# Where the last slice of v, the bias split and batch 1's turns stand in a fused attention and mixer kernel

## The chip, the cores and the metric

One core of a Trainium2 chip runs the whole kernel. The metric is the time of one execution on the device in microseconds (us); three executions of the kernel before were timed, and one more was profiled.

## What is computed

Four batches of 576 tokens, 8 heads of 64: attention with a local mask (heads 0 to 3, the last 32 positions) and a strided mask (heads 4 to 7, every 32nd position), then a gated mixer, then a second mixer with sines and cosines. All in fp32 at the interface.

```python
scores = np.where(masks, scale * q @ k.T, -1e9)      # per head
x = softmax(scores) @ v                              # heads side by side: x is 576 x 512
h = np.maximum(x @ w_in, 0.0)
u, v = h[..., :512], h[..., 512:]
v_n = (v - mean(v)) / np.sqrt(var(v) + 1e-06)
v_s = einsum('ts,bsd->btd', w_spatial, v_n) + b_spatial[None, :, None]
x = (u * v_s) @ w_out
theta = x @ w_theta
y = einsum(w_tok_r, x * cos(theta)) + einsum(w_tok_i, x * sin(theta))
out = x + y + np.maximum((x + y) @ w_ch, 0.0)
```

## The kernel before

Numbers are split in two fp16 halves, high and low (`dst[0]`, `dst[1]`; `e` is the half), and each product is three matmuls, high by high, low by high and high by low (`PASS`). Weights arrive as raw 64-bit words and are converted in steps of two row blocks: a load, two casts on ACT, one operation on DVE, a cast to the high half on ACT and a subtraction for the low half on POOL or DVE (`from_f64`, `steps_w`, `part`).

Batch 0 opens alone with `attention0`: nine groups of score blocks pass through a pipeline of a few steps, `s`. A group is scored on PE (`gr_scores`), shifted on DVE (`gr_shift`: a maximum, TENSOR_REDUCE, and a subtraction, TENSOR_TENSOR), exponentiated on ACT (`gr_exp`), turned by PE transposes and copied by ACT (`gr_turn`, into `pT`), multiplied by v and divided (`gr_pv`), turned back and written to `xT` by ACT and DVE, high half and low half (`gr_out`, `gr_parts`). During this stage each engine takes its instructions in the order in which the code is written.

After it a scheduler sets the order on each engine from priorities, and the main products run in chunks. `main_v` makes v of x @ w_in: four blocks of 128 tokens in two pairs (`v0`, `v1`) and a tail of 64 tokens that PE makes as two halves (`v2`, `tail_mm`, `fold_tail`). `v_relu` evicts a pair or the tail on ACT and takes its statistics on DVE (BN_STATS); `norm` makes 1/sqrt(var) by twelve small DVE operations on the tile `rs` and scales; `norm_q` writes the halves of `vn`. `main_mid` makes four chunks of u (24 matmuls each), four of sp (the product with w_spatial: 24 matmuls and 4 with the tail rows and the bias), of x2 and of th; `main_end` makes y and c. PSUM gives the main chunks and the score tiles of batch 1 (`a`) one pool of three tiles (`pm`).

Batch 1's attention runs beside batch 0's main products. `attention1` is a generator: one step scores group s, sends it through maximum, subtraction and exponential, then turns group s-1 and divides group s. Whenever a main chunk yields, `others()` steps it if the count of main products so far (`now()`, in us of full-clock matmul time) has passed `ATT_AT[b]`, a start and a gap. So a step's instructions on PE (scores, turns, products with v) stand between two chunks, and the turn stands directly behind the scores, with no main products in between.

The last row of `wspt` holds the bias, split in two halves: `sp_tail` loads it behind the tail of w_spatial in `x2f`, and makes two ACT operations of one partition by 576 and one on DVE. `x2f` is afterwards the place of the second half of w_out.

Of the kernel before, what the change touches and what calls it, by code (L numbers as in the profile page):

```python
# [21 lines left out]
STRIDE = 32  # L22
# [12 lines left out]
LAG16 = 3  # L35
V_ORDER = (0, 1, 2)
E_WAY = 'aaaadaaadaa'
# [18 lines left out]
LEAD = 3.0  # L56
ATT_AT = (None, (2.7, 4.2), (86.0, 5.4), (174.5, 4.6))
PREP_AT = (112.0, 126.0, 131.0)
# [11 lines left out]
def kernel(  # L70
# [249 lines left out]
    def sp_tail():  # L320
        stg = pair(stage()[0].bitcast(F32), S)
        for j in range(2):
            nc.sync.dma_start(stg[j * TL:(j + 1) * TL, 0, :], w_spT[T0:S, :])
        nc.sync.dma_start(stg[TL:TL + 1, 1, :], b_sp)
        nc.sync.dma_start(stg[96:97, 1, :], b_sp)
        nc.scalar.activation(wspt[:, 0, :], stg[:, 0, :], AF.Copy, scale=SPS)
        nc.vector.scalar_tensor_tensor(wspt[0:TL, 1, :], stg[0:TL, 0, :], SPS, wspt[0:TL, 0, :],
                                       op0=ALU.mult, op1=ALU.subtract)
        nc.scalar.activation(wspt[TL:TL + 1, 1, :], stg[TL:TL + 1, 1, :], AF.Copy, scale=SPS)
        nc.scalar.activation(wspt[96:97, 1, :], stg[96:97, 1, :], AF.Copy, scale=SPS)  # L330
        nc.vector.scalar_tensor_tensor(wspt[96:97, 1, :], stg[96:97, 1, :], SPS, wspt[96:97, 1, :],
                                       op0=ALU.mult, op1=ALU.subtract)
# [296 lines left out]
    def gr_parts(b, local, blocks, xt, by=1):  # L629
# [3 lines left out]
        for i, (hp, blk) in enumerate(blocks):  # L633
            if runs and runs[-1][0] == hp and (local or blk < 10):
                runs[-1][3] += 1
            else:
                runs.append([hp, blk, i, 1])
        for hp, blk, i, n in runs:
            src = xt[:, QB * i:QB * (i + n)]
            if local:  # L640
                dst = [xh[:, e, hp, QB * blk:QB * (blk + n)] for e in range(2)]
# [11 lines left out]
    def attention0(aside):  # L653
# [12 lines left out]
        nc.scalar.activation(x2f[:, 0, 0:1], halfpi, AF.Exp)  # L666
        make_masks()
        load_qk(0, 0, q[0], k[0], 4 * QB, S)
        load_vl(0, 0, v[0])
# [8 lines left out]
        for s in range(NG + 3):  # L678
            mid, end = aside.get(s, ((), ()))
            if s < NG:  # L680
                if s % 4 == 3:
                    banks = pa("sc"), pa("av")
                else:
                    two = pm("at")
                    banks = two[:, 0, :], two[:, 1, :]
                t = s2("smx")
                sm, pT = t[:, 0, 0:384], t[:, 1, 0:512].rearrange("p (n k) -> p n k", n=4)
                st = att_p.tile([P, 2, 6], F32, tag="st", name="st", bufs=4)
                un[s] = banks, sm, pT, st
                gr_scores(s, q, k, banks[0])  # L690
                gr_shift(s, banks[0], sm, st)
# [125 lines left out]
    def attention1(b):  # L817
# [20 lines left out]
        for s in range(NQ + 2):  # L838
# [17 lines left out]
            if s in loads:  # L856
                f, hp = loads[s]
                f(hp)
            if 1 <= s < NQ:
                turn()  # L860
# [119 lines left out]
    def main_v(b):  # L980
# [43 lines left out]
        def v_mm(ps, i, c):  # L1024
            for n, (xe, we) in enumerate(PASS):
# [3 lines left out]
                    start=(c == 0 and n == 0), stop=(c == NC - 1 and n == 2)).ins.name))  # L1029

        if b == 0:
            ps = [pm("v0")]
# [13 lines left out]
            some(1, (2,))  # L1046
            yield
            for pr in range(2):
                some(pr, (3,))
                yield  # L1050
                v_relu(pr, ps[pr])
            norm((0, 1))
        for pr in V_ORDER if b else V_ORDER[2:]:
            ps = pm(f"v{pr}")
            if pr == 2:
                tail_mm(ps[:, 0, :], xh, win, slice(DM, 2 * DM))
                yield
            else:
                for t in range(2):
                    for c in range(NC):  # L1060
                        v_mm(ps[:, t, :], 2 * pr + t, c)
                    yield
            v_relu(pr, ps)
        norm((2,) if b == 0 else (0, 1, 2))

    def main_mid(b):
# [3 lines left out]
        def u_chunk(m):  # L1070
            ps = pm(f"u{m}")
            k = 0
            for c in range(NC):
                for we, xe in PASS:
                    mm2(ps, win[:, we, c, m * P:(m + 1) * P], xh[:, xe, c, :], k == 0, k == 3 * NC - 1)
                    k += 1
            u = s1(f"u{m}")
            ha.activation(fold(u), halves(ps), AF.Relu, scale=XS / (PS * SS))
            us[m] = u

        def sp_chunk(m):
# [3 lines left out]
            for c in range(NF):  # L1085
                for ve, we in PASS:
                    mm2(ps, vn[:, c, ve, d], wsp[:, we, c, :], k == 0, False)
                    k += 1
            mm2(ps, vn[:, 4, 0, d], wspt[:, 0, :], False, False)
            mm2(ps, k2[:, d], wspt[:, 1, :], False, True)  # L1090
# [4 lines left out]
        for f, m in ((u_chunk, 0), (u_chunk, 1), (u_chunk, 2), (sp_chunk, 0), (u_chunk, 3), (sp_chunk, 1),  # L1095
                     (sp_chunk, 2), (sp_chunk, 3)):
            f(m)
            yield
# [19 lines left out]
        for m in (2, 3):  # L1118
            ps = pm(f"x2{m}")
            x2_mm(m, ps, range(NC))  # L1120
            x2_evac(m, ps)
# [132 lines left out]
    att = {"b": 1, "n": 0}  # L1254

    def now():
        return clock[0] / 2400.0
# [9 lines left out]
    def others():  # L1267
        while conv and conv[0][0] <= now():
            conv.pop(0)[1]()
        while att["b"] < B and ATT_AT[att["b"]][0] + att["n"] * ATT_AT[att["b"]][1] <= now():  # L1270
            step()
# [18 lines left out]
    def go():  # L1290
# [11 lines left out]
        NG + 1: ((), (go, e2, a3, b3)),  # L1302
        NG + 2: ((), (go, c3, lambda: sp_part(0), e3, step, lambda: sp_part(2))),
    })
# [95 lines left out]
```

## Time and profile before

| | |
|---|---|
| time of three executions | 489.02, 491.31 and 491.95 us, median 491.31 |
| time of the profiled execution | 488.88 us |
| its span, first to last instruction | 487.0 us |
| PE busy | 467.9 us (96% of the span) |
| DVE, ACT, POOL busy | 300.2, 268.6, 72.4 us |
| granted TensorE clock, mean | 0.996 |

A row of the timeline gives the start, the length, the engine, the operation, output<-input and, in square brackets, how long the engine had stood before and what ended that. Successive like instructions are merged (x4). PE's matmuls and its weight loads (PEld) are two rows of one engine.

### The profile page before, as it was taken

To read this page: it belongs to the slowest core of one execution; us is meant where nothing else is said; L and a number is where in the kernel's file an instruction comes from. 1 tells how busy PE (TensorE), PEld (TensorE's weight loads), DVE (VectorE), ACT (ScalarE), POOL (GpSimd) and SP (SyncE) were. 2 spreads that over 40 slices of the span, in tenths; PEclk is the share of its full clock that TensorE was granted. 3 is DMA by queue.
4 is the path that set the end of the run, shared out by engine and by line. 5 is a ranking of instruction groups with operands and counts; after the bars stand their busy time and mean duration, and the time that the engine had idled before them with its cause. 6 is when DMAs were issued, how large, how long until landed. Compare 5 with 4: busy or idle time off the path is not lost. (4 is left out here: it accounts for less than half of the span.)

```text
span 487.0 us, 10793 instructions
## 1 busy us (share of the span) xinstructions
PE 467.9 (96%) x4440; PEld 351.5 (72%) x4440; DVE 300.2 (62%) x652; ACT 268.6 (55%) x480; POOL 72.4 (15%) x68
## 2 busy tenths in 40 slices
PE   6889998899999999999999999999999999999996
PEld 5665666677577778777568777777567777777775
DVE  3766997955998546752787878762686121227412
ACT  2668878788954334455945667754942022149202
POOL 2043025120015100201005110111005200210320
PEclk8999999999999999999999999999999999999999
DMA  6989446558860155100381345330450020003502
GB/s 177 288 260 286 187 138 217 171 182 243 158 153 1 63 168 147 54 1 2 85 216 53 88 125 159 66 44 1 68 127 2 1 98 0 1 2 74 122 0 99
DMA packets 71820, 52.72 MB, mean 108 GB/s; under 512 B 50584, under 2 KB 59992, under 8 KB 71770
## 3 DMA queue, kind: packets, MB, share of 16 engines
q1 hardware_dynamic: 71466, 51.42, 38.5%
q8 instruction: 35, 0.57, 0.5%
q10 hardware_dynamic: 304, 0.61, 0.4%
q14 instruction: 15, 0.12, 0.1%
HBM read 35.36 MB, written 4.72 MB: 82 GB/s over the span
## 5 line engine op out<-in xcount | busy, mean ns | idle before, releaser
L107 PE MATMUL y<-wtok,zf 128*128 128x288 f16 x864 | 107.2, 286 | 0.0
L107 PEld LDWEIGHTS <-zf 128*128 128x128 f16 x864 | 84.1, 98 | 22.2 <-issue 1.2
L107 PE MATMUL sp<-wsp,vn 128*128 128x288 f16 x384 | 50.7, 286 | 1.2 <-ACT u L107 1.2
L107 PE MATMUL x<-zf,wout 128*128 128x288 f16 x384 | 49.6, 287 | 0.0
L107 PE MATMUL v<-win,xT 128*128 128x512 f16 (+1 forms) x240 | 48.7, 380 | 0.9 <-DVE xT L107 0.6
L107 PE MATMUL u<-xT,win 128*128 128x288 f16 x384 | 49.2, 286 | 0.0
L107 PEld LDWEIGHTS <-vn 128*128 128x128 f16 x416 | 40.3, 98 | 11.4 <-issue 1.4
L107 PE MATMUL th<-x2h,wth 128*128 128x288 f16 x384 | 47.9, 286 | 0.0
L107 POOL TENSOR_TENSOR x2h<-x2f,x2h 128x576 f16<-128x576 f32 x19 | 26.2, 1382 | 142.4 <-issue 66.1
L107 PE MATMUL c<-x2h,wch 128*128 128x288 f16 x360 | 45.2, 286 | 0.0
L107 PEld LDWEIGHTS <-wth 128*128 128x128 f16 x384 | 37.6, 98 | 9.7 <-issue 0.2
L107 PEld LDWEIGHTS <-wch 128*128 128x128 f16 x384 | 37.4, 98 | 9.2
L107 PEld LDWEIGHTS <-win 128*128 128x128 f16 x384 | 37.4, 98 | 9.1
L107 PEld LDWEIGHTS <-wout 128*128 128x128 f16 x384 | 36.7, 98 | 9.5
L107 PEld LDWEIGHTS <-xT 128*128 128x128 f16 (+1 forms) x240 | 21.1, 100 | 24.9 <-issue 2.2
L107 ACT ACTIVATE x2h<-x2f 128x576 f16<-128x576 f32 (+1 forms) x28 | 20.9, 747 | 24.8 <-DVE x2f L107 23.5
L107 ACT ACTIVATE o<-c 128x576 f32<-128x576 f32 x15 | 9.7, 644 | 34.9 <-PE c L107 34.7
L107 DVE TENSOR_TENSOR ta<-ta,x2f 128x1152 f32<-128x1152 f32 (+1 forms) x17 | 21.7, 1284 | 11.2 <-ACT ta L107 11.2
L107 DVE SCALAR_TENSOR_TENSOR x2f<-y,x2f 128x576 f32<-128x576 f32 x16 | 12.0, 752 | 25.4 <-PE y L107 25.3
L107 POOL TENSOR_TENSOR zf<-u,zf 128x576 f16<-128x576 f32 x8 | 10.2, 1278 | 115.3 <-ACT zf L107 115.3
L107 DVE SCALAR_TENSOR_TENSOR o<-x2f,o 128x576 f32<-128x576 f32 (+1 forms) x17 | 12.2, 722 | 23.6 <-ACT o L107 23.6
L107 DVE TENSOR_TENSOR u<-u,sp 128x576 f32<-128x576 f32 x16 | 12.0, 750 | 22.2 <-PE sp L107 22.2
(144 smaller groups left out, 724.4 us busy)
## 6 DMA issues: line engine op xcount, KB each, us to landing
out_dram<-o SPq DMA_DIRECT2D x15, 288.0 KB
kt<-in_qp_dram SPq DMA_DIRECT2D x8, 288.0 KB
qs<-in_qd_dram SPq DMA_DIRECT2D x8, 288.0 KB
x2f<-in_w_in_dram SPq DMA_DIRECT2D x2, 1024.0 KB
zf<-in_w_in_dram SPq DMA_DIRECT2D x2, 1024.0 KB
xT<-in_w_ch_dram SPq DMA_DIRECT2D x2, 1024.0 KB
kt<-in_kzl_dram SPq DMA_DIRECT2D x8, 152.0 KB
ks<-in_kl_dram SPq DMA_DIRECT2D x4, 304.0 KB
```

The costliest lines, as they stand in the source:

```text
L107: ins = f(*args, **kwargs)
```

## The change

Six edits. (1) `main_v` of batch 0 makes and evicts the tail between the last products of v0 and those of v1, and one `norm` of all five slices follows; before, `norm((0, 1))` came ahead of the tail and `norm((2,))` behind it. (2) The bias gets a tile of its own, is loaded by two DMAs on POOL's queue at the start, and is split in step 1 of `attention0`. (3) `gr_parts` writes two blocks of neighbouring heads in one operation where they lie alike. (4) `attention1` yields for batch 1 between the scores and the turn, so that a step has two parts, timed by `ATT1_AT` (start, gap, distance of the second part). (5) For batch 0 the chunks u and sp yield at half, and the last two x2 chunks too, so that a part can stand in the middle of a chunk. (6) The opening takes two of batch 1's parts in its last step.

```diff
@@ constants @@
-ATT_AT = (None, (2.7, 4.2), (86.0, 5.4), (174.5, 4.6))
+ATT1_AT = (6.9, 4.2, 1.4)
+ATT_AT = (None, None, (86.0, 5.4), (174.5, 4.6))
@@ sp_tail @@
-        nc.sync.dma_start(stg[TL:TL + 1, 1, :], b_sp)
-        nc.sync.dma_start(stg[96:97, 1, :], b_sp)
...
-        nc.scalar.activation(wspt[TL:TL + 1, 1, :], stg[TL:TL + 1, 1, :], AF.Copy, scale=SPS)
-        nc.scalar.activation(wspt[96:97, 1, :], stg[96:97, 1, :], AF.Copy, scale=SPS)
-        nc.vector.scalar_tensor_tensor(wspt[96:97, 1, :], stg[96:97, 1, :], SPS, wspt[96:97, 1, :],
+
+    def bias_load():
+        t = s1("bias")
+        for r in (TL, 96):
+            nc.gpsimd.dma_start(t[r:r + 1, :], b_sp)
+        return t
+
+    def bias_part(t):
+        for r in (TL, 96):
+            nc.scalar.activation(wspt[r:r + 1, 1, :], t[r:r + 1, :], AF.Copy, scale=SPS)
+        nc.vector.scalar_tensor_tensor(wspt[96:97, 1, :], t[96:97, :], SPS, wspt[96:97, 1, :],
                                        op0=ALU.mult, op1=ALU.subtract)
@@ gr_parts @@
+            elif runs and runs[-1][0] == hp - 1 and runs[-1][1] == blk and runs[-1][3] == 1:
+                runs[-1][4] = 2
             else:
-                runs.append([hp, blk, i, 1])
+                runs.append([hp, blk, i, 1, 1])
...
+            if heads == 2:
+
+                src = src.rearrange("p (h c) -> p h c", h=2)
+                dst = [xh[:, e, hp:hp + 2, :] for e in range(2)]
...
@@ attention0 @@
         make_masks()
+        bias = bias_load()
...
+            if s == 1:
+                bias_part(bias)
@@ attention1 @@
                 f(hp)
+            if b == 1:
+                yield
             if 1 <= s < NQ:
                 turn()
@@ main_v, batch 0 @@
-            for pr in range(2):
-                some(pr, (3,))
-                yield
-                v_relu(pr, ps[pr])
-            norm((0, 1))
...
+            some(0, (3,))
+            yield
+            v_relu(0, ps[0])
+            for _ in tail():
+                yield
+            some(1, (3,))
+            yield
+            v_relu(1, ps[1])
...
-        norm((2,) if b == 0 else (0, 1, 2))
+        norm((0, 1, 2))
@@ main_mid: u_chunk and sp_chunk @@
                     k += 1
+                if b == 0 and c == 1:
+                    yield
@@ main_mid: x2, m = 2 and 3 @@
-            x2_mm(m, ps, range(NC))
+            x2_mm(m, ps, (0, 1))
+            if b == 0:
+                yield
+            x2_mm(m, ps, (2, 3))
@@ planner @@
+    def att_due():
+        if att["b"] == 1:
+            s, part = divmod(att["n"] - 1, 2)
+            return ATT1_AT[0] + s * ATT1_AT[1] + part * ATT1_AT[2]
+        start, gap = ATT_AT[att["b"]]
+        return start + att["n"] * gap
...
-        NG + 2: ((), (go, c3, lambda: sp_part(0), e3, step, lambda: sp_part(2))),
+        NG + 2: ((), (go, c3, lambda: sp_part(0), e3, step, step, lambda: sp_part(2))),
```

What this does to the order of instructions is shown at three places. First, DVE in steps 0 and 1 of `attention0`: the first pair is the maximum and the subtraction of group 0, the last pair those of group 1.

```order
 L107 TENSOR_REDUCE st<-at 128x4
 L107 TENSOR_TENSOR smx<-at,st 128x384
+L107 SCALAR_TENSOR_TENSOR wspt<-bias,wspt 1x576
 L107 TENSOR_REDUCE st<-at 128x4
 L107 TENSOR_TENSOR smx<-at,st 128x384
```

DVE's share of the bias split stands ahead of group 1's maximum. On ACT, at the same place, the row above is the exponential of group 0 and the two below are the copy of its turned block and the exponential of group 1.

```order
 L107 ACTIVATE smx<-smx 128x384
+L107 ACTIVATE wspt<-bias 1x576 x2
 L107 ACTIVATE smx<-at 96x512
 L107 ACTIVATE smx<-smx 128x384
```

The two bias operations follow group 0's exponential, and DVE's operation needs the second of them. Second, ACT where it writes the high halves of `vn`, before: `vn<-vr_629` and `vr_651` are the two pairs, `vr_718` the tail, `u_857` the eviction of the third u chunk.

```order
L107 ACTIVATE x2h<-zf 128x1024
L107 ACTIVATE vn<-vr_629 128x2x512
L107 ACTIVATE vn<-vr_651 128x2x512
L107 ACTIVATE u_857<-u_832 128x576
L107 ACTIVATE x2f<-x2f 128x1024
L107 ACTIVATE x2h<-x2f 128x1024
L107 ACTIVATE vn<-vr_718 64x512
```

And now: `vr_631` and `vr_685` are the pairs, `vr_655` the tail, `u_842` the eviction of the third u chunk, `u_805` that of the second.

```order
L107 ACTIVATE x2f<-x2f 128x1024
L107 ACTIVATE u_805<-u_753 128x576
L107 ACTIVATE sm<-sm 128x192
L107 ACTIVATE pT_669<-av 96x512
L107 ACTIVATE wout<-x2h 128x1024
L107 ACTIVATE x2h<-x2f 128x1024
L107 ACTIVATE vn<-vr_655 64x512
L107 ACTIVATE vn<-vr_631 128x2x512
L107 ACTIVATE vn<-vr_685 128x2x512
L107 ACTIVATE u_842<-u_817 128x576
```

The halves of `vn` come behind the conversion of w_out's first half, and the third u chunk is evicted behind all of them. Third, PE at the first sp chunk, now: `a_865` are the scores of batch 1's group 3, `av` the turn of group 2, `u_921` the fourth u chunk.

```order
L107 MATMUL a_865<-mask_100,identb 128x96
L107 MATMUL av<-ident,sm 96x128 x2
L107 LDWEIGHTS vn
L107 MATMUL sp_881<-wsp,vn 128x288
L107 LDWEIGHTS vn
L107 MATMUL sp_881<-wsp,vn 128x288
L107 LDWEIGHTS win
L107 MATMUL u_921<-xT_94,win 128x288
L107 LDWEIGHTS win
L107 MATMUL u_921<-xT_94,win 128x288
L107 LDWEIGHTS vn
L107 MATMUL sp_881<-wsp,vn 128x288
```

Before, the first sp chunk stood directly behind group 3's scores, and group 2's turn in the fourth u chunk; now that turn and two matmuls of the fourth u chunk stand at the head of the first sp chunk.

## Rows read from the trace of the kernel before

**Rows 1.** Windows: length, then busy PE, PEld, DVE, ACT, POOL; clock, DMA share, GB/s.

```profile
48.00:62.00 14.00, 12.48 (x145) 9.43 (x138) 13.94 (x50) 11.79 (x17) 0.00 (x0) 1.00 0.50 187
62.00:77.00 15.00, 14.44 (x179) 10.56 (x177) 13.85 (x29) 11.79 (x20) 6.95 (x6) 1.00 0.55 178
77.00:90.00 13.00, 11.54 (x178) 8.82 (x178) 11.38 (x20) 9.73 (x14) 4.93 (x4) 1.00 0.59 195
90.00:108.00 18.00, 15.72 (x162) 11.75 (x160) 12.39 (x29) 14.57 (x26) 2.73 (x2) 1.00 0.57 184
108.00:132.00 24.00, 23.98 (x160) 14.71 (x159) 19.02 (x22) 22.73 (x30) 0.00 (x0) 1.00 0.79 187
```

**Rows 2.** Timeline of PE, 48 to 105 us: the chunks that stood before they began.

```profile
48.47 3.47 PE L107 MATMUL u<-xT,win 128*128 128x288 f16 x27
...
61.51 1.63 PE L107 MATMUL sp<-wsp,vn 128*128 128x288 f16 x12 [1.25 <-ACT u L107]
...
69.22 0.40 PE L107 MATMUL av<-ident,sm 128*96 128x128 f32 x2 [0.46 <-DVE sm L107]
...
78.53 0.61 PE L107 MATMUL av<-ident,sm 128*96 128x128 f32 x4 [1.08 <-DVE sm L107]
...
85.02 0.63 PE L107 MATMUL av<-ident,sm 128*128 128x128 f32 x4 [0.38 <-DVE sm L107]
...
93.55 0.65 PE L107 MATMUL av<-ident,sm 128*128 128x128 f32 x4 [1.67 <-DVE xT L107]
...
101.04 0.44 PE L107 MATMUL av<-pT,v 54*64 54x54 f32 x8 [0.59 <-ACT pT L107]
```

**Rows 3.** Timeline of batch 0's attention, groups 0 and 1, 9 to 12 us.

```profile
9.23 0.52 ACT L107 ACTIVATE smx<-smx 128x384 f32<-128x384 f32 x1 [5.33 <-DVE smx L107]
9.70 0.56 DVE L107 TENSOR_REDUCE st<-at 128x4 f32<-128x384 f32 x1 [0.51 <-PE at L107]
10.29 0.56 DVE L107 TENSOR_TENSOR smx<-at,st 128x384 f32<-128x384 f32 x1
11.42 0.51 ACT L107 ACTIVATE smx<-smx 128x384 f32<-128x384 f32 x1
11.98 0.64 PE L107 MATMUL at<-ident,smx 128*96 128x128 f32 x4
```

**Rows 4.** Timeline: the bias split where it stood before.

```profile
52.89 0.68 ACT L107 ACTIVATE wspt<-x2f 1x576 f16<-1x576 f32 x1
54.53 0.76 DVE L107 SCALAR_TENSOR_TENSOR wspt<-x2f,wspt 1x576 f16<-1x576 f32 x1
```

**Rows 5.** Timeline of POOL and of SP's queue: POOL's last mask work, and one load.

```profile
3.86 0.25 POOL L107 MEMSET wtok<- 128x18 f32 x4
29.47 1.14 POOL L107 CAST mask<-mf 128x512 bf16<-128x512 f32 x1 [25.35 <-DMA mf<-in_mask_dram]
26.60 0.45 SPq L107 DMA_DIRECT2D mf<-in_mask_dram  x1
```

**Rows 6.** Timeline: the second of two x writes of group 2, and PE behind it.

```profile
21.86 0.22 ACT L107 ACTIVATE xT<-at 128x64 f16<-128x64 f32 x1 [1.21 <-DVE xT L107]
22.40 0.34 PE L107 MATMUL at<-mask,identb 128*128 128x384 bf16 x1 [0.91 <-DVE xT L107]
```

**Rows 7.** Timeline: eviction and fold of v's tail, and four steps of norm.

```profile
48.90 0.59 ACT L107 ACTIVATE vr<-v 64x512 f32<-64x512 f32 x1
49.60 0.65 DVE L107 TENSOR_TENSOR vr<-v,vr 64x512 f32<-64x512 f32 x1
55.92 0.42 DVE L107 TENSOR_TENSOR rs<-rs 128x4 f32<-128x4 f32 x4
```

**Rows 8.** Timeline of DVE: conversion of the second half of w_theta.

```profile
95.25 1.21 DVE L107 SCALAR_TENSOR_TENSOR x2h<-x2f,x2h 128x1024 int32<-128x1024 int32 x1
```

**Rows 9.** Windows of the opening, columns as in rows 1.

```profile
5.00:8.00 3.00, 1.48 (x20) 1.05 (x22) 0.13 (x1) 0.00 (x0) 0.00 (x0) 1.00 0.83 207
8.00:12.00 4.00, 3.79 (x32) 2.41 (x31) 2.28 (x5) 1.52 (x3) 0.00 (x0) 0.57 0.70 165
```

More of the change, by code (lines that the diff above doesn't have):

```diff
@@ L35 @@
 LAG16 = 3
-V_ORDER = (0, 1, 2)
 E_WAY = 'aaaadaaadaa'
@@ L633, in gr_parts @@
         for i, (hp, blk) in enumerate(blocks):
-            if runs and runs[-1][0] == hp and (local or blk < 10):
+            if runs and runs[-1][0] == hp and runs[-1][4] == 1 and (local or blk < 10):
                 runs[-1][3] += 1
-            else:
-                runs.append([hp, blk, i, 1])
-        for hp, blk, i, n in runs:
-            src = xt[:, QB * i:QB * (i + n)]
-            if local:
+            elif runs and runs[-1][0] == hp - 1 and runs[-1][1] == blk and runs[-1][3] == 1:
+                runs[-1][4] = 2
+            else:
+                runs.append([hp, blk, i, 1, 1])
+        for hp, blk, i, n, heads in runs:
+            src = xt[:, QB * i:QB * (i + n * heads)]
+            if heads == 2:
+                src = src.rearrange("p (h c) -> p h c", h=2)
+                dst = [xh[:, e, hp:hp + 2, :] for e in range(2)]
+                if local:
+                    dst = [d[:, :, QB * blk:QB * (blk + 1)] for d in dst]
+                else:
+                    nr = min(3, STRIDE - 3 * blk)
+                    dst = [d.rearrange("p h (j r) -> p h j r", r=STRIDE)[:, :, :, 3 * blk:3 * blk + nr] for d in dst]
+                    src = src[:, :, 0:nr * NCLS].rearrange("p h (r j) -> p h j r", j=NCLS)
+            elif local:
                 dst = [xh[:, e, hp, QB * blk:QB * (blk + n)] for e in range(2)]
@@ L1029, in v_mm, with tail @@
                     start=(c == 0 and n == 0), stop=(c == NC - 1 and n == 2)).ins.name))
+        def tail():
+            ps = pm("v2")
+            tail_mm(ps[:, 0, :], xh, win, slice(DM, 2 * DM))
+            yield
+            v_relu(2, ps)
         if b == 0:
@@ L1047, in main_v @@
             yield
-            for pr in range(2):
-                some(pr, (3,))
-                yield
-                v_relu(pr, ps[pr])
-            norm((0, 1))
[L1053 to L1058, printed above, removed]
+            some(0, (3,))
[6 more added lines that the diff above has]
+            v_relu(1, ps[1])
+        else:
+            for pr in range(2):
+                ps = pm(f"v{pr}")
                 for t in range(2):
@@ L1062, in main_v @@
                     yield
-            v_relu(pr, ps)
-        norm((2,) if b == 0 else (0, 1, 2))
+                v_relu(pr, ps)
+            for _ in tail():
+                yield
+        norm((0, 1, 2))
     def main_mid(b):
@@ L1076, in u_chunk @@
                     k += 1
+                if b == 0 and c == 1:
+                    yield
             u = s1(f"u{m}")
@@ L1088, in sp_chunk @@
                     k += 1
+                if b == 0 and c == 1:
+                    yield
             mm2(ps, vn[:, 4, 0, d], wspt[:, 0, :], False, False)
@@ L1096, in main_mid @@
                      (sp_chunk, 2), (sp_chunk, 3)):
-            f(m)
+            for _ in f(m):
+                yield
             yield
@@ L1119, in main_mid @@
             ps = pm(f"x2{m}")
-            x2_mm(m, ps, range(NC))
+            x2_mm(m, ps, (0, 1))
+            if b == 0:
+                yield
+            x2_mm(m, ps, (2, 3))
             x2_evac(m, ps)
@@ L1269, in others @@
             conv.pop(0)[1]()
-        while att["b"] < B and ATT_AT[att["b"]][0] + att["n"] * ATT_AT[att["b"]][1] <= now():
+        while att["b"] < B and att_due() <= now():
             step()
```

## The prediction

> **What bounds the kernel now.** I read the windows by stage first [rows 1]: there the reader sees PE busy for 12.48 of 14.00, 14.44 of 15.00, 11.54 of 13.00 and 15.72 of 18.00 us, and then 23.98 of 24.00. So behind 108 us PE waits for nothing, and whatever the change does must come from the stretch before. Between 48 and 108 us PE stands for 1.52 + 0.56 + 1.46 + 2.28 = 5.82 us. The same rows show why: DVE is busy for 13.94 of 14 and 13.85 of 15 us. Next, PE's own timeline [rows 2], where the bracket names what ended each stop: 1.25 us at the first sp chunk (ACT's eviction of a u chunk), 0.46, 1.08 and 0.38 at turns of batch 1 that wait for the division on DVE, 1.67 put down to DVE's x write, 0.59 for ACT's copy `pT`. That is 5.43 of the 5.82. Last, the opening [rows 3]: group 1's turn on PE at 11.98 waits for an exponential on ACT, and that for a subtraction on DVE. Here each engine hands work to the next, and a late link makes all later ones late.
>
> The two orders hold the same number of main products on PE, and from th on PE's rows are the same. The time changes by what happens to the opening, and by which of the stops go, stay or are new. One part does less than its name: on PE the tail's 12 matmuls stand behind v1's last five, as before; what moves is the eviction on ACT and the statistics on DVE.
>
> **Bias in attention 0.** The split costs two ACT operations of 0.68 and one DVE operation of 0.76 us [rows 4]. They leave the stretch in which DVE is full, and they enter the opening. There ACT has them behind group 0's exponential, which ends at 9.23 + 0.52 = 9.75 [rows 3]; two more, each starting about 0.6 behind the last, end near 11.1. DVE's operation needs the second one and stands ahead of group 1's maximum, so that starts at 11.1 + 0.76 = 11.9 and not at 9.70. Maximum and subtraction (0.56 each) end at 13.0, and group 1's exponential starts at 13.05 instead of 11.42: 1.6 us late. Behind it on PE wait group 1's turn, group 0's product with v and the scores of group 3, and through them every later group. I find no work in the opening that waits for something of its own and so would take this up; cost +1.6, bounds +1.2 (a slack of 0.4 later in the chain) and more than +1.6 if the load lands late (first rival).
>
> The loads themselves move from SP to POOL, ahead of the memsets for which SP's loads of v wait. No row shows POOL issuing a DMA. The nearest is SP's issue, 0.45 us for one [rows 5]; two would put the memsets off by 0.9, at the other end I allow 1 us each. SP's loads then run some 1 to 2 us late, and the attention chain that uses them runs 1.6 late by itself, so I add nothing.
>
> **Merged x writes.** In group 2 the second write on ACT stood 1.21 us for the first one's DVE half, and PE behind it stood 0.91 [rows 6]. One write of two heads saves a DVE operation and the round trip: PE starts some 0.4 earlier. The like pair of groups 5 to 8 gives 0.2. Sum -0.6 (bounds 0 and -1.0). In batches 1 and 2 they lie beside PE's work: nothing. The opening together: +1.6 - 0.6 = +1.0.
>
> **The tail's eviction.** Before, the first u chunk started at 48.47 without a stop [rows 2], on a PSUM tile that ACT had freed. Now it takes the tail's tile, which is free when DVE has folded the tail. ACT reaches the tail 0.9 earlier than 48.90, since one pair is now evicted behind it (a half of ACT's work there); the fold, 0.65 [rows 7], then ends near 49.3, and PE starts at 49.35: a new stop of +0.9. It is 1.8 if ACT stays at 48.90 and the fold at 49.60, and 0 if PE comes later by itself.
>
> **One norm for five slices.** Twelve steps for four columns and twelve for one become twelve for five: 12 x 0.42 / 4 = 1.3 us less on DVE [rows 7], and with the bias (0.76) 2.0 us less where it is full. But now all scaling waits for the last pair's statistics, the high halves of `vn` come on ACT behind the casts of w_out, and the eviction of the third u chunk comes behind the three `vn` casts. PE reaches the first sp chunk with three waits in a row: the division of group 2 ahead of its turn (0.4), `vn` (0.2), and for the two matmuls of the fourth u chunk the PSUM tile that the late eviction frees (1.1). Sum 1.7 in place of 1.25. Bounds 0 (DVE's 2.0 us arrive in time) and 3.2 (each of the three half a us longer, about one DVE operation of 0.56 [rows 3]).
>
> **Turns half a step later.** Between a group's scores and its turn there now stand 12 or 24 main products, 1.5 to 3 us at 3.47 / 27 each [rows 2]. The stops of 0.46 and 1.08 us are shorter than that: I take both as gone. The stop of 0.38 stays and grows to 0.5, that of 1.67 goes down to 1.0, that of 0.59 to 0.3, because the turn there waits for a DVE that works without a gap and not only for the step before it; and the conversion of w_theta's second half, 1.21 us of DVE at 95.25 [rows 8], now stands in DVE's order ahead of the division of group 5, whose turn was at 85.02 [rows 2], since its load is issued earlier. Bounds of the three together: 0 (as meant) and 4.0 (the 1.21 and ACT's conversions come on top of what they were).
>
> **The sum.** Stops before 5.43; after 0.9 + 1.7 + 0.5 + 1.0 + 0.3 = 4.4; difference -1.0. With the opening, +1.0 - 1.0 = 0.0. The profiled execution took 488.88 us, 2.43 less than the median of the three timed ones, 491.31; a change of nothing puts the new median at 491.3. What can be told from no change here is about 1%, 4.9 us, since three executions alone lie 2.9 apart.
>
> **Rival: the bias lands late, and the opening pays.** ACT and DVE stop in their order until the two loads of the bias are there. POOL is free for them at 3.9 [rows 5]; they are wanted at 9.75, so 5.8 us is the point from which it decides, and from there each us is a us for the whole kernel. Against it: a 256 KB load on SP took 29.47 - 26.60 = 2.9 us from issue to use [rows 5]. For it: a load from POOL appears nowhere in this trace, and the queues are in use (DMA share 0.83 [rows 9]). If it takes 3 us more than wanted, the opening costs 1.0 + 3.0. The clock may add to it: PE was busy for 1.48 of 3.00 us, and then in 8 to 12 us its granted clock averaged 0.57 [rows 9], so most of that stretch ran at the lower level, 1.2 GHz. A stop of several us just there may bring this back; the 3.79 busy us of that window could be about 1.6 less at the full clock, and I take 1 us for a second such stretch. Without the gain of the middle: 491.3 + 3.0 + 1.0 = 495.3, slower. The Trainium skill ("SBUF — State Buffer", SBUF: two separate sides) has a rule that speaks for it: the descriptors of a load issued on POOL are written by GpSimd, and DVE can shut it out of the port they share for a whole instruction. The row shows DVE busy for 0.13 of 3.00 us from 5 to 8 [rows 9], so by that rule there is little to be shut out by. The Trainium skill ("TensorE: Matmul & The Clock Gate", Part 1) says that lack of activity throttles PE and activity releases it; the trace agrees, with 0.57 after the half idle window, and by it the extra stop would cost more than the stop alone.
>
> **Rival: the turns really are hidden.** DVE has 2.0 us less to do between 48 and 73, and every stop from 69 on waits for DVE or for ACT behind it. If all of them go, only the new stops 0.9 and 1.25 stay: 5.43 - 2.15 = 3.3 less. With a bias split that finds more slack than I saw (+0.8 and the merges' -0.6, +0.2) the time is 491.3 - 3.1 = 488.2. Against it stands DVE's share of 11.38 of 13 and 12.39 of 18 us in the later windows [rows 1]: there is less slack than the stops suggest.
>
> **Rival: one conversion takes the place of another.** The second half of w_theta, moved ahead of the turns of groups 5 and 6, holds DVE for 1.21 us and ACT for about three casts, and each turn behind it is late by this: +2 on the three last stops, 493.3.
>
> **Chances.** The forecast 0.42; hidden turns 0.24; late bias 0.18; conversion 0.16. Only the best part of the second case goes below 486.4 (faster by over 1%): it wants all of the 5.43 gone, the two new stops too; 0.09. Only the worst part of the late bias goes above 496.2: 0.07. Within 1%: 0.84. The range runs from the second case less the spread of the timed runs downwards, 488.2 - 2.3 = 485.9, to the late bias, 495.3.
>
> **What would show it.** Right: in the new profile the exponential of group 1 starts near 13.05 and PE's first v matmul about 1 us later than before; a stop of near 1 us stands ahead of the first u chunk; the stops of 0.46 and 1.08 are gone; those at the last turns are still there; th begins within 1 us of its old place. Wrong: an opening that is as long as before (then the slack was there, and the gain of the middle shows), a wait of ACT for the bias load, a granted clock under 1 behind 12 us, or a PE that runs from 69 us to th without a stop.

## The result, and the profile after

The changed kernel took 496.06 us (median of six, 495.05 to 497.49); the kernel before, six times beside it, 490.88. The ratio is 1.0119, 95% interval 1.0097 to 1.0142: slower by 1.2%. The forecast was 491.3 with a range up to 495.3, so the result lies outside it, and "slower by over 1%" had been given 0.07. The profiled execution took 497.26 us with a span of 495.5; that of before had 487.0. The profiled execution of before (488.88) was faster than its six timed ones and this one is nearly the slowest of its six, so of the 8.5 us between the spans some 3 belong to the executions and not to the change; the medians differ by 5.2.

First the windows of the changed kernel, columns as in rows 1.

```profile
8.00:12.00 4.00, 4.00 (x32) 2.58 (x30) 1.12 (x3) 1.90 (x4) 0.00 (x0) 1.00 0.77 171
12.00:20.00 8.00, 6.26 (x61) 4.70 (x59) 4.53 (x11) 2.78 (x7) 0.00 (x0) 1.00 1.00 305
48.00:62.00 14.00, 13.21 (x131) 8.98 (x129) 13.39 (x39) 10.64 (x15) 2.27 (x2) 1.00 0.56 192
62.00:77.00 15.00, 11.49 (x97) 7.79 (x96) 13.82 (x24) 12.18 (x17) 4.97 (x5) 0.77 0.36 112
77.00:90.00 13.00, 12.71 (x166) 10.00 (x166) 9.60 (x17) 8.55 (x13) 6.20 (x6) 1.00 0.81 287
90.00:108.00 18.00, 14.00 (x205) 10.65 (x202) 16.11 (x29) 11.29 (x19) 2.02 (x2) 1.00 0.62 191
108.00:132.00 24.00, 23.64 (x209) 17.08 (x208) 16.27 (x22) 23.00 (x35) 0.00 (x0) 1.00 0.49 139
```

Against [rows 1] one window stands out: 62 to 77, where PE is busy for 11.49 us and not 14.44, at a granted clock of 0.77 and not 1.00 (part of it at the lower level, 1.2 GHz). Next PE's timeline of the changed kernel: the places of [rows 2], and two of the opening.

```profile
6.83 1.54 PE L107 MATMUL at<-kt 64*64 64x96 f32 x14 [0.21 <-DMA kt<-in_kzl_dram]
...
14.54 1.09 PE L107 MATMUL at<-ident,smx 128*96 128x128 f32 x4 [1.74 <-ACT smx L107]
...
36.13 1.46 PE L107 MATMUL v<-win,xT 128*128 128x512 f16 x6 [1.51 <-DVE xT L107]
...
53.20 1.63 PE L107 MATMUL u<-xT,win 128*128 128x288 f16 x12 [0.64 <-DVE vr L107]
...
68.77 0.63 PE L107 MATMUL av<-ident,sm 128*96 128x128 f32 x2 [2.91 <-DVE sm L107]
70.23 0.64 PE L107 MATMUL u<-xT,win 128*128 128x288 f16 x2 [0.35 <-ACT u L107]
71.11 4.64 PE L107 MATMUL sp<-wsp,vn 128*128 128x288 f16 x22 [0.24 <-DVE vn L107]
...
94.08 0.63 PE L107 MATMUL av<-ident,sm 128*128 128x128 f32 x4 [1.42 <-DVE sm L107]
102.79 0.66 PE L107 MATMUL av<-ident,sm 128*128 128x128 f32 x4 [2.46 <-DVE xT L107]
...
115.53 5.06 PE L107 MATMUL th<-x2h,wth 128*128 128x288 f16 x40
```

The first v matmul and th stood here before, on PE's timeline:

```profile
31.39 1.24 PE L107 MATMUL v<-win,xT 128*128 128x512 f16 x5 [0.56 <-DVE xT L107]
...
107.69 12.10 PE L107 MATMUL th<-x2h,wth 128*128 128x288 f16 x96
```

So v is 4.7 us late, th 7.8, and behind th only 0.7 more is lost (the spans end 8.5 apart). The stops of 0.46 and 1.08 in [rows 2] are gone; that of 1.25 at the first sp chunk has become 2.91 + 0.35 + 0.24, and the 22 sp matmuls behind it take 4.64 us at the lower clock. So 4.7 us are lost in the opening and 3.1 between the first u, which is 4.7 late as well, and th. Last, what PE waits for at 68.77: DVE and POOL on the timeline of the changed kernel.

```profile
64.02 4.33 DVE L107 TENSOR_SCALAR vr<-vr,mv,rs 128x512 f32<-128x512 f32 x5
64.81 2.52 POOL L107 TENSOR_TENSOR wout<-x2h,wout 128x512 f16<-128x512 f32 x2 [13.81 <-ACT wout L107]
68.28 0.34 DVE L107 TENSOR_TENSOR sm<-sm,st 128x192 f32<-128x192 f32 x1
```

And the scalings by the view of the tile `vr`, 44 to 72 us (count, then the least, median and most ns of one), now and before:

```profile
L107 DVE TENSOR_SCALAR vr<-vr,mv,rs x5: 534/822/1383, 64.0 to 67.5; 128x512 f32<-128x512 f32 x4, 64x512 f32<-64x512 f32 x1
```

```profile
L107 DVE TENSOR_SCALAR vr<-vr,mv,rs x5: 529/541/543, 57.5 to 63.0; 128x512 f32<-128x512 f32 x4, 64x512 f32<-64x512 f32 x1
```

Before, no scaling took more than 543 ns, and four in a row took 1.91 us. Now five take 4.33, and the division of group 2 (68.28), for which PE stands, is queued behind them. POOL makes the low halves of w_out's first half beside them.

### The profile page after: what moved, and what is told of

Same layout as the page of the kernel before. It is cut to its first block, busy times and chain, and to the rows that moved or that the text cites. A ratio compares the mean times of both kernels' runs of the same rounds, so it can differ in the third digit from the quotient of the medians.

```text
span 495.5 us, 10767 instructions
## 1 busy us (share of the span) xinstructions
PE 472.3 (95%) x4440; PEld 355.4 (72%) x4440; DVE 304.2 (61%) x630; ACT 267.6 (54%) x470; POOL 70.9 (14%) x70
## 5 line engine op out<-in xcount | busy, mean ns | idle before, releaser
L107 PE MATMUL sp<-wsp,vn 128*128 128x288 f16 x384 | 52.2, 293 | 0.2 <-DVE vn L107 0.2
L107 PE MATMUL v<-win,xT 128*128 128x512 f16 (+1 forms) x240 | 48.5, 380 | 1.5 <-DVE xT L107 1.5
L107 PEld LDWEIGHTS <-vn 128*128 128x128 f16 x416 | 41.3, 100 | 11.6 <-DVE vn L107 0.8
L107 PE MATMUL x<-zf,wout 128*128 128x288 f16 x384 | 49.4, 286 | 0.0
L107 ACT ACTIVATE x2h<-x2f 128x576 f16<-128x576 f32 (+1 forms) x28 | 20.9, 748 | 26.9 <-DVE x2f L107 26.5
L107 ACT ACTIVATE o<-c 128x576 f32<-128x576 f32 x15 | 9.7, 645 | 34.9 <-PE c L107 34.7
```

Source lines behind the costliest of these rows:

```text
L107: ins = f(*args, **kwargs)
```

## Experiments

Three theories. **Opening**: the bias split in step 1 makes everything late, by the held chain and by a clock that is at its lower level behind it. **Collision**: the one norm puts five scalings and group 2's division in one row on DVE, beside POOL's low halves of w_out; DVE's operations last longer beside POOL's, PE stands, and its clock falls. **Turns**: the half-step turns lose by themselves. The table has every run: the time, its ratio to before in the same comparison, and where PE's first v, first u and th stand in its profile (before: 31.4, 48.5, 107.7; changed: 36.1, 53.2, 115.5). Run 11 has times only.

| run | us | ratio, 95% | v, u, th |
|---|---|---|---|
| 1 bias alone | 494.28 | 1.0082, 1.0053 to 1.0110 | 35.3, 51.9, 112.4 |
| 2 bias back | 491.05 | 1.0012, 0.9992 to 1.0033 | 31.9, 48.9, 110.0 |
| 3 norm alone | 496.27 | 1.0141, 1.0113 to 1.0170 | 32.3, 49.8, 113.8 |
| 4 norm back | 493.76 | 1.0079, 1.0049 to 1.0109 | 35.6, 51.8, 112.5 |
| 5 turns alone | 496.46 | 1.0123, 1.0066 to 1.0181 | 31.4, 49.9, 113.7 |
| 6 turns back | 496.53 | 1.0130, 1.0086 to 1.0174 | 35.9, 53.0, 114.8 |
| 7 bias, turns back | 495.20 | 1.0122, 1.0065 to 1.0178 | 31.2, 49.9, 113.8 |
| 8 bias, norm back | 494.90 | 1.0102, 1.0065 to 1.0140 | 31.4, 49.1, 112.3 |
| 9 bias in step 11 | 497.10 | 1.0143, 1.0108 to 1.0178 | 31.7, 51.9, 114.9 |
| 10 opening filled | 496.83 | 1.0129, 1.0086 to 1.0171 | 33.4, 51.7, 115.8 |
| 11 run 10, halves on DVE | 491.75 | 1.0042, 1.0016 to 1.0068 | |
| 12 changed, halves on DVE | 491.69 | 1.0034, 1.0007 to 1.0060 | 34.9, 52.0, 110.0 |
| 13 norm alone, halves on DVE | 490.67 | 1.0021, 1.0008 to 1.0035 | 31.7, 49.8, 110.7 |
| 14 turns alone, halves on DVE | 493.26 | 1.0067, 1.0040 to 1.0093 | 34.1, 50.8, 110.3 |
| 15 bias back, halves on DVE | 490.43 | 1.0007, 0.9982 to 1.0032 | 31.4, 50.7, 109.3 |
| 16 before, halves on DVE | 492.85 | 1.0057, 1.0036 to 1.0078 | 32.8, 49.4, 111.3 |
| 17 run 15, warm start | 490.82 | 1.0020, 0.9989 to 1.0051 | 31.2, 49.9, 108.5 |
| 18 before, merges, halves, warm | 491.18 | 1.0020, 0.9991 to 1.0048 | 31.7, 48.6, 107.6 |

**One part alone, one part back (runs 1 to 8).** Run 1 puts the hunks `sp_tail` and `attention0` of the change into the kernel before:

```diff
+        bias = bias_load()
...
+            if s == 1:
+                bias_part(bias)
```

> The kernel before with the bias move alone. If it is the opening that pays for it, the first v matmul is at 35 to 36 us (31.39) and the time is 3.5 to 5 us above before, 494 to 496, less at most 1 for DVE in 48 to 62. Rival: bias and clock have nothing to do with each other: the move costs the held chain alone, 1.6 us by the forecast, 492 to 493.

Its opening, by the timeline of ACT, DVE and PE:

```profile
9.70 1.38 ACT L107 ACTIVATE wspt<-bias 1x576 f16<-1x576 f32 x2
11.12 0.75 DVE L107 SCALAR_TENSOR_TENSOR wspt<-bias,wspt 1x576 f16<-1x576 f32 x1 [2.00 <-ACT wspt L107]
13.08 0.52 ACT L107 ACTIVATE smx<-smx 128x384 f32<-128x384 f32 x1 [1.38 <-DVE smx L107]
13.66 1.09 PE L107 MATMUL at<-ident,smx 128*96 128x128 f32 x4 [1.74 <-ACT smx L107]
```

And by the windows, columns as in rows 1:

```profile
8.00:12.00 4.00, 3.68 (x30) 2.22 (x28) 1.94 (x4) 2.47 (x4) 0.00 (x0) 0.54 0.68 168
12.00:20.00 8.00, 6.29 (x74) 5.04 (x74) 4.44 (x13) 3.08 (x7) 0.00 (x0) 0.59 1.01 298
```

Group 1's exponential starts at 13.08; 13.05 was forecast. But PE, which has stood 1.74 us for it, goes on at the lower level: the transposes take 1.09 and not 0.64 [rows 3], and from 12 to 20 us the granted clock is 0.59. The clock fell ahead of the stop, as before the change (0.54 here from 8 to 12 us, 0.57 in [rows 9]); there it was back by 11.98 us, and here it was not. The first v matmul is 3.9 us late: 1.6 of chain; the rest is put down to the clock, which run 10 tries. Run 2 takes the same hunks out of the changed kernel:

> The changed kernel with the bias's load and split back behind the tail of w_spatial (SP's queue, x2f). If the split in step 1 of attention 0 is what makes the opening late, group 1's exponential is back near 11.4 us (13.96 changed), the first v matmul near 31.4 (36.13) and the time falls by some 4 to 5 us, to 491 to 492, or less if the 1.4 us of bias work in the full stretch costs something there. Rival: the matmuls that run at half rate from 6 to 19 us in the changed kernel are a matter of the clock alone, and come without the bias too: then the first v matmul stays behind 33 and the time behind 494.

v is back at 31.9, and 5.0 us are gone. So the bias is the loss of the opening, with and without the other parts: with the split in step 1 the table has v at 34.9 to 36.1 (33.4 in run 10, with its stop filled), without it at 31.2 to 32.8, save in run 14. In run 2's trace too the first scores run at the lower level, and PE, which did not stand, is at the full one by 12.7 us. Run 14's 34.1 has another source: in its trace PE stands 2.44 us ahead of 20.9 for an x write, which follows two conversions on ACT.

Runs 3 and 4 put the hunk `main_v` into the kernel before and take it out of the changed one:

```diff
-            norm((0, 1))
...
-        norm((2,) if b == 0 else (0, 1, 2))
+        norm((0, 1, 2))
```

> The kernel before with the tail between the pairs and one norm for five slices alone. If the norm makes the collision by itself, two or three of the five scalings take 1.4 us beside POOL's halves of w_out, a stop of 2 us or more stands at the first sp chunk or at group 2's turn, the clock falls behind it, and the time is 3 to 6 us above before: 493 to 496. Rival: without the late turns the scalings come earlier than ACT's cast of w_out, no collision: 489 to 491.

> The changed kernel with main_v of batch 0 as before: norm of four slices ahead of the tail, norm of one behind it. If the five scalings in a row (4.33 us beside POOL's halves of w_out) are what holds the division of group 2, the stop of 2.91 at its turn is gone, the clock in 62 to 77 us is 1.00 and not 0.77, and the time falls by 3 to 4 us, to 492 to 493. Rival: the stop is what the later opening and w_out's conversion ask for, and another stop of 2 to 3 us stands in its place: then 495 to 497.

Alone it costs 6.9 us, in a kernel with the old opening and the old turns. Its DVE, POOL and PE:

```profile
60.90 3.21 DVE L107 TENSOR_SCALAR vr<-vr,mv,rs 128x512 f32<-128x512 f32 x5
62.39 2.72 POOL L107 TENSOR_TENSOR wout<-x2h,wout 128x512 f16<-128x512 f32 x2 [14.81 <-ACT wout L107]
64.00 0.42 PE L107 MATMUL sp<-wsp,vn 128*128 128x288 f16 x2 [1.04 <-ACT vn L107]
64.14 1.53 DVE L107 TENSOR_TENSOR vn<-vr,vn 64x512 f16<-64x512 f32 x1
65.78 0.28 PE L107 MATMUL u<-xT,win 128*128 128x288 f16 x1 [1.36 <-ACT u L107]
67.80 3.52 PE L107 MATMUL sp<-wsp,vn 128*128 128x288 f16 x14 [1.73 <-DVE vn L107]
```

The three waits that the prediction named (sp for `vn`, u for its PSUM tile, sp again for `vn`) come to 4.1 us in place of 1.25. Put back in the changed kernel (run 4) it gives 2.3 us.

Runs 5 and 6 do the same with the turns (hunks `attention1`, `main_mid`, planner and constants):

```diff
+            if b == 1:
+                yield
             if 1 <= s < NQ:
                 turn()
```

> The kernel before with batch 1's steps in two parts alone (with the half yields of u, sp and x2 and the second step at the end of the opening). If the half step hides the division, the stops of 0.46 and 1.08 are gone and no other grows: 1.5 to 3 us faster, 488 to 489.5. Rival: what it gains there it gives back at the last turns, where w_theta's second conversion now stands ahead (1.42 and 2.46 in the changed kernel): within 1 us of before. Third: it is what breaks the middle, and the time is 2 to 4 us above before.

> The changed kernel with batch 1's turns as before (steps in one part, no half yields): bias, norm and merged writes alone. By the other runs the turns were worth -4.2 us beside the new norm and without the bias (491.05 against 495.2), so without them this is near 499 to 500. If the late opening takes that up, it is within 1 us of the changed kernel's 496.06; and if the turns are a loss by themselves, 490 to 492.

Alone they cost 6.5 us; taken out of the changed kernel they give nothing. What runs 5 and 3 have in common is the collision. In run 5, by the view of the tile `sm` from 60 to 80 us (ns, as for `vr` above):

```profile
L108 DVE TENSOR_TENSOR sm<-sm,st x2: 345/1710/3074, 68.5 to 71.5; 128x384 f32<-128x384 f32 x1, 128x192 f32<-128x192 f32 x1
```

And by the timeline of POOL and PE:

```profile
67.86 1.12 POOL L108 COPY k<-vn 64x512 f16<-64x512 f16 x1 [18.65 <-ACT vn L108]
68.95 2.25 POOL L108 TENSOR_TENSOR wout<-x2h,wout 128x512 f16<-128x512 f32 x2
71.68 1.09 PE L108 MATMUL av<-ident,sm 128*96 128x128 f32 x4 [2.81 <-DVE sm L108]
```

One division of 0.55 us took 3.07: it began beside POOL's copy of `k` and ended behind both halves of w_out.

Runs 7 and 8 put two parts back, leaving the norm, or the turns, with the merged writes.

> The changed kernel with bias and turns as before: tail, one norm and merged x writes alone (the half yields of u, sp and x2 are out too). If the late turns are a loss (6.5 us when they were put into the kernel before alone), this is well under 491.05: 486 to 489. If the norm is the loss (2.3 us when it was put back in the changed kernel), it is 491 to 493. If each of the two needs the other, it is above 493.

> The changed kernel with bias and norm as before: half-step turns and merged x writes alone. With the turns' 6.5 us standing by themselves, 495.5 to 496.5; if the loss of the turns came from where DVE's division fell beside POOL's halves of w_out (3.07 us for one division, else 0.55), a small shift in the opening can move it: then anything from 490 to 493, and that division is short in this trace. If merged writes are worth 0.6 us, that is all that they can explain.

Both stay 5 us above before, though without the moved bias; with norm and turns together and without the bias (run 2) it was 1.0. Run 8 repeats run 5: a division of 3.08 us beside POOL, and a stop of 2.81 behind it. In run 7 the five scalings are undisturbed (2.36 us); the tail's subtraction behind them takes 1.42 and a scaling of two columns 1.02, both beside POOL's halves of w_out (0.98 and 0.17 in run 13, which has none of them on POOL), and the three waits come to 3.8. So the parts do not add, and the long operation is another one from kernel to kernel.

**The opening (runs 9, 10).** Run 9 keeps the load on POOL and moves the split, run 10 puts seven products of the identity into the stop of 1.74 (each is two records):

```diff
-            if s == 1:
+            if s == NG + 2:
                 bias_part(bias)
```

```diff
+            if s == 2:
+                fil = pa("av")
+                for _ in range(7):
+                    nc.tensor.matmul(fil[:, 0:P], ident, ident, start=True, stop=True)
```

> The changed kernel with the bias split in step 11 of attention 0 (near 33 us, where ACT and DVE stand for more than half of the time) in place of step 1; its load stays on POOL's queue at the start. If the place in step 1 is what costs, the first v matmul is back near 31.5 to 32 us and the time near 491.0, as with the bias put back (491.05) or up to 1.4 us better, since DVE and ACT keep the gain in 48 to 62 us. Rival: POOL's issue of the loads, ahead of its memsets and so of SP's loads of v, is part of it: then the first v matmul stays 1 us or more behind 32 and the time above 492.

> The changed kernel with 7 more products of the identity on PE, into a PSUM tile that nobody reads, in the stop ahead of group 1's turn (14.54 us, where PE stood 1.74). If the opening loses two things, the held chain and then a clock at its lower level because PE stood, the transposes and products behind the stop run at 0.64 and not 1.09, the first v matmul comes 1.5 to 2.5 us earlier than 36.13 and the time falls by as much, to 493.5 to 494.5. Rival: the lower level is there whatever PE does in the stop: no change, 496, or up to 0.5 us more for the filling.

In run 9 v is back at 31.7, so POOL's issue of the loads costs v next to nothing. But the split in step 11 is in the way there (ACT makes it from 42.83 to 44.21, then the x write for which PE stands), and two stops of 1.76 and 1.11 us stand among v's products:

```profile
44.65 0.60 PE L107 MATMUL v<-win,xT 128*128 128x512 f16 x2 [1.76 <-ACT xT L107]
48.93 2.24 PE L107 MATMUL v<-win,xT 128*64 128x512 f16 x15 [1.11 <-DVE sm L107]
```

Run 10 tries the clock of the opening. PE and DVE:

```profile
12.55 1.93 PE L107 MATMUL av<-ident 128*128 128x128 f32 x14
14.49 0.65 PE L107 MATMUL at<-ident,smx 128*96 128x128 f32 x4
...
33.42 1.24 PE L107 MATMUL v<-win,xT 128*128 128x512 f16 x5 [0.55 <-DVE xT L107]
...
62.63 4.33 DVE L107 TENSOR_SCALAR vr<-vr,mv,rs 128x512 f32<-128x512 f32 x5
67.38 0.50 PE L107 MATMUL av<-ident,sm 128*96 128x128 f32 x2 [2.97 <-DVE sm L107]
```

With PE kept busy the transposes behind the stop take 0.65 and not 1.09, and v comes 2.7 us earlier. Yet the end does not move: the collision follows as before (4.33, a stop of 2.97), and th stays at 115.8. The first u is 1.5 us earlier and th 0.3 later, so the middle loses 1.7 more, and the lower clock accounts for it: the 22 sp matmuls take 5.12 and not 4.64, and 18 x2 matmuls behind the stop of 2.46 take 3.82 and not 2.37.

**The collision (runs 11 to 16).** One edit takes POOL out of it: DVE makes w_out's low halves itself.

```diff
-    timed(sq_parts(wout, w_out), *CONV_OUT)
+    timed(sq_parts(wout, w_out, 2), *CONV_OUT)
```

> The run with the filled opening (496.83), with the low halves of w_out made on DVE in place of POOL (four operations of 128x512). If the long stop at group 2's turn (2.97) comes from POOL's two halves of w_out, beside which three of DVE's five scalings took 1.38, 1.37 and 0.82 us in place of 0.53, the scalings take 2.7 us together, that stop falls to 1 to 1.5, the lower clock behind it is gone, and th comes 2 to 5 us earlier: 492 to 495. Rival: DVE is full there and the four operations (0.6 to 0.7 us each) take back what POOL no longer costs: 496 to 498.

> The changed kernel with the low halves of w_out on DVE and nothing else. If POOL's halves beside the scalings, and the clock behind that stop, are the loss of the middle, and the opening's 4.7 us reach the end once the middle has no such stop, this is 491.9 + 2.3 to 2.7 = 494.0 to 494.6. If the middle alone was the loss and the opening is taken up by later stops, 491.5 to 492.5. If POOL's halves are worth nothing without the filling, 496.

> The same with the low halves of w_out on DVE. If the collision is the norm's loss, the scalings take 2.4 to 2.7 us together and the time is 2 us or more under that of the run before, and at or under 492.85, what the halves on DVE cost without the norm: 489 to 492. If the norm loses by its order alone (vn late on ACT), the time stays where the run before is.

> The kernel before with the half-step turns alone (496.46), with the low halves of w_out on DVE. There one division took 3.07 us in place of 0.54 beside POOL's halves, PE stood 2.81 for it and the clock was at its lower level for 6.8 us behind. If that one division is the loss, it is 0.54 here and the time falls by 3 to 6 us, to 490.5 to 493.5. Rival as in the run before: DVE's four more operations make another stop, 495 to 497.

> The changed kernel with the bias put back (491.05), with the low halves of w_out on DVE. Its scalings are the same five beside POOL's halves (1.39 and 1.37), and PE stood 2.76 behind them for vn. If POOL is the cause, the stop falls to about 1.2, the later ones of 2.07 and 1.56 do not grow, and the time is 1 to 3 us less, 488 to 490, which would be under before. Rival: DVE pays for it, 491 to 493.

> The kernel before with the low halves of w_out on DVE. Its excess on DVE beside POOL was 2.19 us only, none of it at a long stop, so within 1 us of 489.9, and a little above if DVE is the fuller engine there (490 to 491.5). Then what is left to the half-step turns, with the halves on DVE, is 493.26 less this: about 2 to 3 us, the opening's accident of that run among it. Rival: it gains 1 to 2 us too (488 to 489), and the turns cost 4 to 5 without POOL.

In the changed kernel it gives 4.4 us (run 12), beside the norm alone 5.6 (13), beside the turns alone 3.2 (14). Run 12's timeline, where the order up to the stop of 0.62 is that of the changed kernel:

```profile
62.51 2.35 DVE L107 TENSOR_SCALAR vr<-vr,mv,rs 128x512 f32<-128x512 f32 x5
65.27 0.40 PE L107 MATMUL av<-ident,sm 128*96 128x128 f32 x2 [0.62 <-DVE sm L107]
67.29 0.64 PE L107 MATMUL u<-xT,win 128*128 128x288 f16 x2 [1.06 <-ACT u L107]
68.04 4.04 PE L107 MATMUL sp<-wsp,vn 128*128 128x288 f16 x22
```

The same five scalings in 2.35 us, the stop 0.62 and not 2.91. With the order of DVE and ACT unchanged up to there, that shows the collision at this place. The three waits there come to 1.8 us and not 3.5, and the stops of the later turns fall as well, by 2.2 in all. The lower clock, though, stays for the most part: the 22 sp matmuls take 4.04 and not 4.64 (2.87 at the full level in run 2), and in run 13, where two stops of 1.06 are the longest of that place, the granted clock from 62 to 77 us is again 0.77. So the clock of that stretch is not the collision's alone. Between the first u and th there were 62.3 us in the changed kernel and are 58.0 now; with the norm alone 64.0 and 60.9, with the turns alone 63.8 and 59.5, with the bias back 61.1 and 58.6. Only in the kernel before, which has no such collision, it costs: 59.2 and 61.9 (run 16), in all 3.0 us. There POOL meets another division of batch 1, and PE stands for that one:

```profile
86.39 1.68 POOL L107 TENSOR_TENSOR zf<-u,zf 128x576 f16<-128x576 f32 x1 [1.48 <-ACT zf L107]
86.86 1.76 DVE L107 TENSOR_TENSOR sm<-sm,st 128x512 f32<-128x512 f32 x1
88.77 1.09 PE L107 MATMUL av<-ident,sm 128*128 128x128 f32 x4 [2.68 <-DVE sm L107]
```

With the halves on DVE the other sums change too: the turns cost 493.26 - 492.85 = 0.4 us and not 6.5, the norm alone gains 492.85 - 490.67 = 2.2 where it cost 6.9, and the moved bias costs 491.69 - 490.43 = 1.3 and not 5.0. For the last the traces show where an early v loses its lead: in run 15 v starts 3.6 us earlier than in run 12 and u only 1.3, with stops of 0.60 and 0.30 for `win` from POOL, 0.56 for ACT's `xT` and 1.01 ahead of u. Filling the opening (run 11 against 12) is worth nothing at the end. All these are differences of medians from different comparisons, in which the kernel before itself stands at 489.4 to 490.9; they are good to about 1 us.

**The search for a version faster than both (runs 17, 18).** A warm start (16 products of the identity in place of 6), on run 15 and on the kernel before with merged writes and the halves on DVE.

```diff
-WARM = 6
+WARM = 16
```

> The changed kernel with the bias put back and the low halves of w_out on DVE (490.43), with 16 products of the identity at the start in place of 6, which fill PE's stop between 4.3 and 6.9 us. If PE's clock falls in the opening because PE stood there, the scores and turns from 6.8 to 12 us run at the full level (0.87 and 0.64 in place of 1.54 and 1.09), v starts 1 to 2 us earlier than 31.4 and the time is 488.5 to 489.5. Rival: the lower level comes whatever PE did before, or the chain of loads and DVE decides: 490 to 491.

> The kernel before with merged x writes, the low halves of w_out on DVE and 16 products of the identity at the start: the parts that cost DVE or ACT nothing. Merges -0.6, warm start -1 to -1.5 if the clock is PE's standing, halves 0 to +1: 488 to 490. Rival: the middle falls into another stop, 491 to 495.

By run 17's timeline of PE the scores do run at the full level (0.88 for 16), but they begin at 7.54, behind the products, and not at 5.99 as in run 15, and v is where it was:

```profile
2.16 5.46 PE L107 MATMUL av<-ident 128*128 128x128 f32 x29
7.54 0.88 PE L107 MATMUL at<-kt 64*64 64x96 f32 x16
```

Neither is faster than before; nor was any other run.

## Why the prediction was wrong, point by point

- **One norm for five slices** failed, and the middle is the larger part of the miss: between the first u and th the forecast had stops of 3.5 for 5.43, 1.9 us less, and the profile has 3.1 more. The step put the three waits at the first sp chunk at 1.7 us, with bounds of 0 and 3.2, from DVE's nominal durations. They measured 3.5 (changed) and 4.1 (alone). It counted 2.0 us less work on DVE and did not look at what stands beside the new row of scalings on POOL: the low halves of w_out, 5.6 of the 6.95 us that [rows 1] show for POOL in that window. Beside them the scalings took 4.33 us and not 2.35 (run 12). It had no term for the clock either: behind the stop 22 sp matmuls took 4.64 us where run 2 has 2.87, and most of that stays without the collision. Norm alone costs 6.9 us, without POOL 1.3; put back in the changed kernel it gives 2.3, less than the bias with its 5.0.
- **Bias in attention 0** was right in its chain (13.05 forecast, 13.08 alone; 13.96 in the changed kernel, whose first scores ran at the lower level, as run 2's do without the bias) and mis-sized as a whole: +1.6 was taken, +3.9 measured at v alone and +4.7 changed, because the clock was left to the rival. Alone it costs 4.3 us. The bound "more than +1.6 if the load lands late" named the wrong condition: the loads were there in time, ACT's split follows directly on group 0's exponential (at 9.70 alone), and the clock was at its lower level behind the stop, which filling the stop put right (run 10).
- **The rival that the opening pays** came near in size (495.3 against 496.06) with half of its mechanism: the clock, without a late load. It priced "a second such stretch" at 1 us; filling the stop brought v 2.7 us forward. Its sum has a slip as well: by its own terms (opening 1.0 + 3.0, clock 1.0, no gain of the middle, on 491.3) it is 496.3. That either figure is near is luck: no load was late, and the 3.1 us that the middle lost are in neither.
- **Turns half a step later**: the stops of 0.46 and 1.08 did go. Those said to become 0.5, 1.0 and 0.3 became 1.42, 2.46 and none: 3.9 in place of 1.8, and in the changed kernel the turns are worth nothing (run 6). With the halves on DVE (run 12) the first of these turns has no stop and the second 1.26, with 0.65 at a product with v between them; that the collision hands their length on is argued from this and not shown.
- **The third rival**, a conversion that takes the place of another, has the size of that (+2 on these stops), and its own mechanism is not there. w_theta's second conversion does stand ahead of group 5's division now (DVE, 84.82 us, 1.23 long), but behind it DVE stood idle for 0.70 and 1.13 us before that division (93.25). Directly ahead of it stand the conversion `wx` (1.36) and u's product with sp (0.75), the same two as before (82.25 and 83.53 us).
- **The tail's eviction**: a stop of 0.9 was forecast ahead of the first u chunk, 0.64 is there, for DVE's `vr`. Right.
- **The base** of the forecast, 491.31, was the median of three executions. Six gave 490.88 and the later sets of 8 to 31 gave 489.4 to 490.2, so the change costs more than 496.06 against 491.3 shows.
- **Merged x writes**: [rows 6]'s stop of 0.91 is 0.46 in the changed kernel, as forecast (0.4 earlier). Their share of the time was never measured alone.
- **The port of DVE and POOL**: the Trainium skill ("SBUF — State Buffer", SBUF: two separate sides) was cited for the bias's load, where it decided nothing. The Trainium skill's rule in the same section, that DVE (in some operations, those with two inputs in SBUF among them) and GpSimd (POOL) share a port pair which one of them holds for a whole instruction while the other is blocked, is the one that bears on the collision: the traces agree, with 1.38 us for a scaling of 0.54. The division of 0.55 that took 3.07 waited for more than the one instruction beside which it began.

What stays open: which stops bring the lower clock. In the changed kernel one of 2.91 us did (0.77 from 62 to 77), in run 2 one of 2.76 did not, and in runs 12 and 13 the lower level came behind stops of at most 1.06. The stop of 2.46 at 102 us brought it in run 10 (18 x2 matmuls in 3.82 us) and not in the changed kernel (2.37). Run 2's window, and its 22 sp matmuls behind that stop:

```profile
62.00:77.00 15.00, 9.78 (x95) 7.26 (x95) 14.90 (x22) 11.21 (x16) 6.57 (x6) 1.00 0.51 179
```

```profile
66.88 2.87 PE L107 MATMUL sp<-wsp,vn 128*128 128x288 f16 x22 [0.40 <-DVE vn L107]
```

That an early v waits for w_in was read from the traces and not tried, and the later turns' stops were not taken apart.

## What to carry to other kernels

When an edit puts several DVE instructions in a row, read POOL's timeline over the same stretch before using their durations: a short DVE operation that PE waits for can last longer than POOL's (0.54 us became 1.38, 0.55 became 3.07). A new stop of PE may have to be priced twice, as the stop and as the matmuls behind it at the lower clock. And where an order is packed this closely, test parts in pairs: three parts that each cost 4 to 7 us alone cost 5 together.

## What was not expected of the hardware

- A DVE division of 0.55 us lasted 3.07, past the rest of one POOL instruction and two whole ones of 1.1 us behind it (run 5): it was passed over, not only held up once.
- A stop of 1.74 us in the opening kept PE at the lower level until behind 18 us, and seven products of the identity in it were enough to avoid that (1.09 against 0.65 for the same transposes). In run 6 PE was back at the full level ahead of a stop of 2.62 us (eight score matmuls in 0.55), and the lower one came behind it (1.09).
- The clock column can be silent: in the changed kernel it reads 1.00 from 8 to 20 us, while 16 score matmuls at 16.68 took 1.55 us, and 4 transposes at 14.54 took 1.09, the lengths that both have in run 1, whose column reads 0.59. In the opening the lengths are the better witness.
